# Reordered start, paired score staging and an earlier fold in an attention and max-out kernel on one Trainium2 core

## The chip, the cores and the metric

The kernel runs on one core of a Trainium2 chip. TensorE (PE, with its weight loads shown as PEld) does the matmuls and transposes, VectorE (DVE) and ScalarE (ACT) read their results out of PSUM, GpSimd (POOL) does some element-wise work and issues most transfers, and SyncE (SP) issues the transposing transfers. The metric is the device time of one execution in microseconds; a kernel's time is the median of its runs.

## The reference

For each of four batches, 32 inducing vectors attend to 12,544 rows of x, and the rows then attend to the 32 results. A max-out layer follows.

```python
def mab(q, kv):
    s = scale * (q @ kv.transpose(0, 2, 1))
    s = s - s.max(-1, keepdims=True)
    a = np.exp(s)
    a /= a.sum(-1, keepdims=True) + 1e-09
    return a @ kv
h = mab(I, x)          # x: (4, 12544, 128), I: (4, 32, 128)
y = mab(x, h)          # then flattened to (50176, 128)
out = np.maximum(y @ w1, y @ w2) @ w_out     # w1, w2: 128 x 1024, w_out: 1024 x 128
```

The kernel uses max(a, b) = a + relu(b - a): the part y @ w1 @ w_out goes through one 128 x 128 product w1out = w1 w_out, and only relu(y @ (w2 - w1)) is made in full width. As y is a mixture of the 32 rows of h, both are applied to h first (hwd = h (w2 - w1), m1 = h w1out), and each row of x only mixes 32 rows of these.

## The kernel before, in words

A batch is 98 column groups of 128 rows. **The start** handles batch 0 in eight units (five of 16 groups, one of 2, two of 8): `load_unit` loads a unit as float16, `u_transpose` transposes it on PE (line 194), `u_scores` makes the scores against the inducing vectors (210) and their exp (219), and `u_accum` adds the unit into two PSUM banks, h (234) and the row sums (244). `keep_warm` issues matmuls without use on a buffer of zeros. `prep_w1T` transposes w1 (610) and copies it out (616). `u_h` reduces the sums, takes the reciprocal and makes hT (255, 260, 262). The differences w21 = w2 - w1 are four subtractions (659). Then `small_hwd` makes hwd (354) and `prep_w1out` makes w1out (622).

**The steady part** is one list of bursts, 49 for a batch. The rows of a batch are cut into blocks of 16 groups and some smaller ones: batch 0 has blocks of 2, 4, 8, five times 16, and 4 groups, the others six of 16 and one of 2. A block of 16 takes eight bursts. `Block.stage` makes the exp of a block's scores against h, called e: four matmuls on column quarters of the array (409) and an activation (419). `Part.burst` makes four banks of relu inputs with matmuls on row quarters (474), which DVE (505) or ACT (509) evict as relu, and may open the next finals (489). `Part.final` multiplies relu with w_out (545, sometimes opened by 536), DVE scales by the denominator (561), and every second final issues an output transfer from POOL (569). `dens` makes denominators (430, 439).

Beside the bursts of batch b the sums of batch b + 1 are prepared: `p1_scores` (277, 286) and `p1_accum` (299, 309 or 312 on DVE; 316 or 319 on POOL, into eacc), then `small_fold` (324, a reduction of eacc on DVE), `small_h` (335 on PE, 338, 340), `small_hwd` (354) and `small_m1` (374).

The order on every engine is written out by hand: each engine runs its instructions in the order in which this program emits them. A small planner (`Model`) keeps estimated times of PE, DVE and ACT and chooses which of DVE and ACT evicts a bank and which of the eight PSUM banks is used. Its choices fix what is emitted and change nothing while the kernel runs. Work beside the bursts is tied to burst numbers by `at(g, f, ...)`, and a block is staged three bursts before its first burst.

Of the kernel before, what the change touches and what calls it, by code (L numbers as in the profile page):

```python
# [51 lines left out]
def kernel(  # L52
# [9 lines left out]
    nc = tc.nc  # L62
    B, N, C = x.shape
    M = inducing.shape[0]
# [12 lines left out]
        units += [(i, g, min(step, n - g)) for g in range(0, n, step)]  # L77
    units = units[:-3] + units[-1:] + units[-3:-1]
    NU = len(units)
    W_AT = NU - 3  # L80

    consts = ctx.enter_context(tc.tile_pool(name="consts", bufs=1))
    big = ctx.enter_context(tc.tile_pool(name="big", bufs=1))
# [11 lines left out]
    model = Model()  # L95
    uid = [0]

    def bank(shape, dtype=F32):
        i = model.bank()
        uid[0] += 1  # L100
        return i, psum.tile(shape, dtype, name=f"ps{uid[0]}", tag=f"bank{i}", bufs=1)
# [8 lines left out]
    def xn_of(b, i):  # L110
        return xn_tiles[(NP1 * b + i) % NXN]

    def load_x(b, i):
        k0, n = p1_blocks[i]
        nc.gpsimd.dma_start(out=xn_of(b, i)[:, 0:n, :], in_=xr[b, :, k0 : k0 + n, :])  # L115

    def load_unit(i):
        t, g, n = units[i]
        k0 = p1_blocks[t][0] + g
        nc.gpsimd.dma_start(out=xn_of(0, t)[:, g : g + n, :], in_=xr[0, :, k0 : k0 + n, :])  # L120
# [21 lines left out]
    identity16 = consts.tile([128, 128], F16, name="identity16")  # L142
    identity32 = consts.tile([128, 128], F32, name="identity32")
# [6 lines left out]
    w1f, w2f = wf[:, 0, :], wf[:, 1, :]  # L150
# [6 lines left out]
    with tc.manual_schedule(engines={ET.PE, ET.DVE, ET.Activation, ET.Pool, ET.SP}):  # L157
# [1 line left out]
        nc.vector.memset(warm, 0.0)  # L159
        nc.vector.memset(ones32, 1.0)  # L160
        nc.vector.memset(ones16, 1.0)
        load_unit(0)
        make_identity(nc, identity16)
        make_identity(nc, identity32)
        for i in range(1, NU):
            if i == W_AT:
                nc.gpsimd.dma_start(out=w1f, in_=moe_w1)
            load_unit(i)
        nc.gpsimd.dma_start(out=w2f, in_=moe_w2)
        nc.gpsimd.dma_start(out=woutp, in_=moe_w_out.rearrange("(jb j) c -> j jb c", j=128))  # L170

        def keep_warm(k):
            bi, ps = bank([128, 512])
            for _ in range(k):
                nc.tensor.matmul(out=ps, lhsT=warm[:, 0:128], rhs=warm, start=True, stop=True)
                end = model.pe(0.215, model.bank_free[bi])
            model.bank_free[bi] = end
# [5 lines left out]
        pool0 = {}  # L183

        def u_transpose(i):
            t, g0, n = units[i]
            xn = xn_of(0, t)
            step = 8 if n == P1B else 4
            for g in range(g0, g0 + n, step):
                m = min(step, g0 + n - g)  # L190
                bi, ps = bank([128, 8, 128], F16)
                end = 0.0
                for j in range(m):
                    nc.tensor.transpose(ps[:, j, :], xn[:, g + j, :], identity16)  # L194
                    end = model.pe(0.056)
                k = p1_blocks[t][0] + g
                dst = xT_tiles[0][:, k : k + m, :]
                if (g // step) % 2 == 0:
                    nc.vector.tensor_copy(out=dst, in_=ps[:, 0:m, :])  # L199
                    model.bank_free[bi] = model.ev("DVE", 64 * m, end)  # L200
                else:
                    nc.scalar.copy(out=dst, in_=ps[:, 0:m, :])  # L202
                    model.bank_free[bi] = model.ev("ACT", 128 * m, end)
# [21 lines left out]
        def u_accum(i):  # L225
            t, g, n = units[i]
            et = pool0.pop(("et", i))
            xn = xn_of(0, t)
            if i == 0:
                for name in ("h", "sum"):  # L230
                    pool0[name] = bank([128, 512])
                    model.bank_free[pool0[name][0]] = 1e9
            for j in range(n):
                nc.tensor.matmul(  # L234
                    out=pool0["h"][1][:, 0:M],
                    lhsT=xn[:, g + j, :],
                    rhs=et[:, j, :],
                    start=(i == 0 and j == 0),
                    stop=(i == NU - 1 and j == n - 1),
                )  # L240
                model.pe(0.025)
            for j in range(0, n, 4):
                w = min(4, n - j) * M
                nc.tensor.matmul(
                    out=pool0["sum"][1][:, 0:w],
                    lhsT=ones16,
                    rhs=et[:, j : j + w // M, :],
                    start=(i == 0 and j == 0),
                    stop=(i == NU - 1 and j + 4 >= n),
                )  # L250
                model.pe(0.056)

        def u_h():
            rec = smp.tile([C, M], F32, name="hrec_0", tag="hrec")
            nc.vector.reduce_sum(
                out=rec,
                in_=pool0["sum"][1][:, 0 : 4 * M].rearrange("p (k m) -> p m k", k=4),
                axis=mybir.AxisListType.X,
            )
            nc.vector.reciprocal(out=rec, in_=rec)  # L260
            hT4 = smp.tile([C, 4, M], F16, name="hT4_0", tag="hT4")
            nc.vector.tensor_mul(  # L262
                hT4,
                pool0["h"][1][:, None, 0:M].broadcast_to((C, 4, M)),
                rec[:, None, :].broadcast_to((C, 4, M)),
            )
            end = model.ev("DVE", 256 + 128, model.t["PE"], 0.2)
            for name in ("h", "sum"):
                model.bank_free[pool0[name][0]] = end
            st[0]["hT4"] = hT4.rearrange("c q m -> c (q m)")  # L270
# [302 lines left out]
        def blocks_of(b):  # L573
            sizes = [16] * (K // 16)
            rest = K - sum(sizes)
            while rest:
                s = 8 if rest >= 8 else 4 if rest >= 4 else 2
                sizes.append(s)
                rest -= s
            if b == 0:  # L580
                sizes = [2, 4, 8] + sizes[:-1]
                sizes[-1] = K - sum(sizes[:-1])
                last = sizes.pop()
                while last:
                    s = 8 if last >= 8 else 4 if last >= 4 else 2
                    sizes.append(s)
                    last -= s
            assert sum(sizes) == K
            res, k0 = [], 0
            for s in sizes:  # L590
                res.append(Block(b, k0, s))
                k0 += s
            return res
# [11 lines left out]
        def prep_w1T():  # L605
            for g in range(2):
                bi, ps = bank([128, 512])
                for j in range(4):
                    jb = 4 * g + j
                    nc.tensor.transpose(  # L610
                        ps[:, 128 * j : 128 * (j + 1)],
                        w1f[:, 128 * jb : 128 * (jb + 1)],
                        identity32,
                    )
                    end = model.pe(0.12, model.bank_free[bi])
                nc.scalar.copy(out=w1T[:, 4 * g : 4 * g + 4, :], in_=ps)
                model.bank_free[bi] = model.ev("ACT", 512, end)
# [16 lines left out]
        for i in range(last):  # L634
# [5 lines left out]
            keep_warm(1)  # L640
        u_scores(last - 1)
        u_accum(last - 2)
        prep_w1T()
        u_transpose(last)
        u_transpose(last + 1)
        u_accum(last - 1)
# [6 lines left out]
        u_accum(last + 2)  # L653
        for i in range(NXN - NP1):
            load_x(1, i)
        for i in range(4):
            eng = nc.vector if i < 2 else nc.gpsimd
            sl = slice(256 * i, 256 * (i + 1))
            eng.tensor_sub(w21[:, sl], w2f[:, sl], w1f[:, sl])
        for i in range(NXN - NP1, NP1):  # L660
            load_x(1, i)
        u_h()
        keep_warm(2)
        flat = [blk for b in range(B) for blk in blocks_of(b)]
        parts = [p for blk in flat for p in blk.parts]
        seq = [(p, u) for p in parts for u in range(p.nburst)]
        first = {}
# [2 lines left out]
            first.setdefault(p.blk.name, g)  # L670

        stages = {}
        for blk in flat:
            stages.setdefault(max(-1, first[blk.name] - 3), []).append(blk)
        stages[-1][0].stage()
        small_hwd(0)
        for blk in stages[-1][1:]:
# [5 lines left out]
        def at(g, f, *a):  # L683
            jobs.setdefault(g, []).append((f, *a))

        for b in range(B - 1):
            nb, g = b + 1, first[b]

            t0, l0 = (9, 24) if b == 0 else (-3, 16)
            at(g + t0, transpose_batch, nb)  # L690
            if nb + 1 < B:
                at(g + l0, hold_loads, nb)
            for i in range(NP1):
                s = g + (14 + 4 * i if b == 0 else 5 + 5 * i)
                at(s, p1_scores, nb, i)
                at(s + 2, p1_accum, nb, i)
                if nb + 1 < B:
                    at(g + l0 + 2 * i, load_x, nb + 1, i)
            for s, f in ((41, small_fold), (42, small_h), (43, small_hwd), (44, small_m1)):
                at(g + s, f, nb)  # L700

        queue = []
# [52 lines left out]
```

## Time and profile before

| | us |
|---|---|
| median of 9 runs | 349.05 |
| lowest and highest run | 348.19 and 351.48 |
| the profiled execution, its whole time | 351.33 |
| the profiled execution, span from the first to the last instruction | 349.2 |

All nine, in order: 348.19, 348.75, 348.84, 348.84, 349.05, 350.72, 350.95, 351.33, 351.48.

| engine | busy us in the span |
|---|---|
| PE | 335.8 |
| PEld | 267.6 |
| DVE | 302.1 |
| ACT | 270.3 |
| POOL | 95.5 |

In lines of the profile, times are microseconds from the first instruction; L12 is line 12 of the kernel before; `out<-in` names tiles without their numbers; x16 is a count of instructions, which can be a little short, as some records are missing. A timeline line gives start, duration, engine, line, operation, tiles and shapes, and in brackets idle time with what ended it. The chain of waits follows the last-ending work back from step to step. Matmuls overlap in the pipeline, so starts are compared with starts.

### The profile page before, as it was taken

The numbers are of one execution on the slowest core, as the hardware profiler recorded it, in microseconds if no ns is written. First come the engines' busy times: TensorE is split into PE (matmuls) and PEld (weight loads), VectorE is DVE, ScalarE is ACT, GpSimd is POOL, SyncE is SP. The second block draws the span as 40 slices with busy tenths as digits, with TensorE's granted clock in tenths as the row PEclk, the third lists the DMA queues.
The fourth block names the chain that finished last, engine by engine and source line by source line (L and its number), as shares of the span: only waits on it lengthen the run. The fifth ranks groups of instructions, "written<-read, shape, count | busy, mean of one in ns | idle before, by whom it ended". The sixth has DMA issues, their size and how long they took to land.

```text
span 349.2 us, 14492 instructions
## 1 busy us (share of the span) xinstructions
PE 335.8 (96%) x6349; PEld 267.6 (77%) x6349; DVE 302.1 (86%) x632; ACT 270.3 (77%) x519; POOL 95.5 (27%) x168
## 2 busy tenths in 40 slices
PE   7787999999999999999999999999999999999994
PEld 3775678888878788887777788887777778777774
DVE  2235899999999899999999999999999999999992
ACT  2465787777888887787888987787888889888980
POOL 6231112346412123544211222324211121111111
PEclk9896899999999999999999999999999999999999
DMA  7999559969947993997218992122212122222222
GB/s 117 232 244 215 133 133 258 197 158 195 213 145 136 222 256 100 179 226 205 92 71 164 254 206 94 68 88 92 92 65 92 77 92 92 95 92 92 93 94 105
DMA packets 51790, 50.42 MB, mean 144 GB/s; under 512 B 41456, under 2 KB 42000, under 8 KB 51728
## 3 DMA queue, kind: packets, MB, share of 16 engines
q0 software_dynamic: 13376, 39.85, 40.8%
q1 hardware_dynamic: 38352, 9.65, 17.0%
q8 instruction: 49, 0.80, 1.0%
q14 instruction: 13, 0.11, 0.1%
HBM read 27.28 MB, written 25.69 MB: 152 GB/s over the span
## 4 chain that ended last, share of the span: by engine, by line
PE 47%; issue 33%; POOL 9%; DMA 4%; DVE 4%; ACT 1%; POOLq 0%; ACTq 0%
PE ps L545 27%; PE ps L474 10%; POOL out_dram L569 7%; DMA xn<-in_x_dram 4%; DVE relu L505 2%; PE ps L489 2%; POOL eacc L319 2%; PE ps L277 1%; PE ps L409 1%; PE ps L299 1%; ACT relu L509 1%; PE ps L234 1%; PE ps L194 1%; DVE o L561 1%; DVE esum L324 1%
## 5 line engine op out<-in xcount | busy, mean ns | idle before, releaser
L509 ACT ACTIVATE relu<-ps 128x512 f16<-128x512 f32 x444 | 235.8, 601 | 47.7 <-PE ps L474 36.6
L505 DVE TENSOR_SCALAR relu<-ps 128x512 f16<-128x512 f32 x340 | 218.9, 680 | 6.5 <-PE ps L474 5.1
L545 PE MATMUL ps<-woutp,relu 128*128 128x128 f16 x3136 | 210.6, 221 | 0.0
L545 PEld LDWEIGHTS <-relu 128*128 128x128 f16 x3136 | 177.7, 98 | 28.7 <-issue 18.9
L569 POOL DMA_DIRECT2D out_dram<-o x100 | 54.4, 544 | 234.2 <-DVE o L561 170.5
L561 DVE TENSOR_TENSOR o<-ps,rp 128x256 f32<-128x256 f32 x196 | 82.0, 418 | 14.6 <-PE ps L545 11.2
L474 PE MATMUL ps<-e,hwd 32*128 32x256 f16 (+1 forms) x1632 | 83.4, 271 | 0.3
L474 PEld LDWEIGHTS <-hwd 32*128 32x128 f16 x1632 | 27.4, 93 | 19.1 <-issue 3.1
L489 PE MATMUL ps<-m,e 32*128 32x128 f16 x372 | 29.4, 214 | 0.4
L489 PEld LDWEIGHTS <-e 32*128 32x128 f16 x372 | 18.2, 92 | 6.7 <-issue 3.2
L319 POOL TENSOR_TENSOR eacc<-eacc,et 128x512 f32<-128x512 f32 (+1 forms) x18 | 18.5, 1029 | 0.3
L419 ACT ACTIVATE e<-ps 128x512 f16<-128x512 f32 (+2 forms) x30 | 16.3, 543 | 2.0 <-PE ps L409 2.0
L202 ACT COPY xT<-ps 128x1024 f16<-128x1024 f16 (+1 forms) x7 | 6.2, 890 | 12.9 <-PE ps L194 12.4
L199 DVE COPY xT<-ps 128x1024 f16<-128x1024 f16 (+2 forms) x8 | 4.5, 575 | 12.8 <-PE ps L194 12.7
L286 ACT ACTIVATE et<-ps 128x512 f16<-128x512 f32 (+1 forms) x21 | 11.4, 544 | 5.0 <-PE ps L277 5.0
L115 POOL DMA_DIRECT2D xn<-in_x_dram x21 | 11.5, 550 | 5.9 <-DMA xn<-in_x_dram 4.6
L409 PE MATMUL ps<-xT,hT 128*32 128x512 f16 (+2 forms) x120 | 11.2, 361 | 0.8 <-DVE hT L262 0.7
L194 PE MATMUL ps<-identity,xn 128*128 128x128 f16 x98 | 7.7, 238 | 3.3 <-DMA xn<-in_x_dram 3.0
L277 PE MATMUL ps<-inducingT,xT 128*128 128x32 f16 x294 | 10.6, 176 | 0.0
L299 PE MATMUL ps<-et,xn 128*128 128x32 f16 x294 | 10.6, 176 | 0.0
L194 PEld LDWEIGHTS <-xn 128*128 128x128 f16 x98 | 6.7, 107 | 4.6 <-DMA xn<-in_x_dram 4.2
L277 PEld LDWEIGHTS <-xT 128*128 128x128 f16 x294 | 9.6, 96 | 0.0
(65 smaller groups left out, 119.1 us busy)
## 6 DMA issues: line engine op xcount, KB each, us to landing
out_dram<-o POOLq DMA_DIRECT2D x96, 256.0 KB, 2.7
xn<-in_x_dram POOLq DMA_DIRECT2D x23, 512.0 KB, 8.6
wf<-in_moe_w_dram POOLq DMA_DIRECT2D x2, 512.0 KB, 14.2
xn<-in_x_dram POOLq DMA_DIRECT2D x2, 256.0 KB, 15.8
out_dram<-o POOLq DMA_DIRECT2D x4, 128.0 KB, 3.7
xT<-xn SPq DMA_TRANSPOSE x21, 6.3
xn<-in_x_dram POOLq DMA_DIRECT2D x4, 64.0 KB, 9.6
woutp<-in_moe_w_out_dram POOLq DMA_DIRECT2D x1, 256.0 KB, 12.5
```

The source lines that it names most:

```text
L194: nc.tensor.transpose(ps[:, j, :], xn[:, g + j, :], identity16)
L277: nc.tensor.matmul(out=ps[:, j * M : (j + 1) * M], lhsT=xT_tiles[b % 2][:, k0 + j, :], rhs=inducingT, start=True, stop=True,)
L319: nc.gpsimd.tensor_add(out=acc, in0=acc, in1=et[:, 0:n, :])
L409: nc.tensor.matmul(out=ps[32 * q : 32 * (q + 1), 0 : self.width], lhsT=st[self.b]["hT4"][:, 32 * q : 32 * (q + 1)], rhs=xT[:, q % self.g], ...
L419: nc.scalar.activation(out=self.e2[:, 0 : self.width], in_=ps[:, 0 : self.width], func=AF.Exp, scale=scale,)
L474: nc.tensor.matmul(out=ps[:, jj * w : (jj + 1) * w], lhsT=st[blk.b]["hwd"][r, 128 * jb : 128 * (jb + 1)], rhs=blk.e2[r, 128 * self.t0 : 12 ...
L489: nc.tensor.matmul(out=part.fin[q][1][:, 128 * s : 128 * (s + 1)], lhsT=part.blk.e2[r, 128 * tt : 128 * (tt + 1)], rhs=st[part.blk.b]["m1" ...
L505: nc.vector.tensor_scalar(out=dst, in0=src, scalar1=0.0, scalar2=None, op0=ALU.max)
L509: nc.scalar.activation(out=dst, in_=src, func=AF.Relu)
L545: nc.tensor.matmul(out=o, lhsT=self.relu[:, jb, q, tt, :], rhs=woutp[:, jb, :], start=False, stop=(s == 1 and jb == NJB - 1),)
L561: nc.vector.tensor_mul(self.osb[:, h : h + 2, :], ps[:, 0:256].rearrange("p (s c) -> p s c", s=2), rp.broadcast_to((128, 2, 128)),)
L569: nc.gpsimd.dma_start(out=outr[blk.b, :, k : k + nst, :], in_=self.osb[:, 0:nst, :])
```

## The change

The start: all eight units of x are loaded ahead of w1, w2 and w_out, where w1 had stood ahead of the last three units. The two identities are made after the third load is issued, not after the first. `u_accum` issues the sums' matmuls ahead of the h matmuls. `prep_w1T` moves from before the last three units to behind `u_h`, in the place of two warm-up matmuls, which are dropped. `u_h` moves ahead of the subtractions and of the later loads, and three of the four subtractions are on POOL instead of two.

The steady part: blocks are staged in pairs, both three bursts before the first burst of the first of them; the first three blocks of batch 0 stay single. `small_fold` is tied to burst 40 of a batch instead of 41.

```diff
-    W_AT = NU - 3
...
-        load_unit(0)
-        make_identity(nc, identity16)
-        make_identity(nc, identity32)
-        for i in range(1, NU):
-            if i == W_AT:
-                nc.gpsimd.dma_start(out=w1f, in_=moe_w1)
+        for i in range(NU):
             load_unit(i)
+            if i == 2:
+                make_identity(nc, identity16)
+                make_identity(nc, identity32)
+        nc.gpsimd.dma_start(out=w1f, in_=moe_w1)
         nc.gpsimd.dma_start(out=w2f, in_=moe_w2)
...
         def u_accum(i):
...
-            for j in range(n):
-                nc.tensor.matmul(out=pool0["h"][1][:, 0:M], ...)
-                model.pe(0.025)
             for j in range(0, n, 4):
                 nc.tensor.matmul(out=pool0["sum"][1][:, 0:w], ...)
                 model.pe(0.056)
+            for j in range(n):
+                nc.tensor.matmul(out=pool0["h"][1][:, 0:M], ...)
+                model.pe(0.025)
...
         u_accum(last - 2)
-        prep_w1T()
         u_transpose(last)
...
         for i in range(NXN - NP1):
             load_x(1, i)
+        u_h()
         for i in range(4):
-            eng = nc.vector if i < 2 else nc.gpsimd
+            eng = nc.vector if i == 3 else nc.gpsimd
             sl = slice(256 * i, 256 * (i + 1))
             eng.tensor_sub(w21[:, sl], w2f[:, sl], w1f[:, sl])
         for i in range(NXN - NP1, NP1):
             load_x(1, i)
-        u_h()
-        keep_warm(2)
+        prep_w1T()
...
-        for blk in flat:
-            stages.setdefault(max(-1, first[blk.name] - 3), []).append(blk)
+        for b in range(B):
+            blks = [blk for blk in flat if blk.b == b]
+            lead_in = 3 if b == 0 else 0
+            for i, blk in enumerate(blks):
+                j = i if i < lead_in else i - (i - lead_in) % 2
+                stages.setdefault(max(-1, first[blks[j].name] - 3), []).append(blk)
...
-            for s, f in ((41, small_fold), (42, small_h), (43, small_hwd), (44, small_m1)):
+            for s, f in ((40, small_fold), (42, small_h), (43, small_hwd), (44, small_m1)):
                 at(g + s, f, nb)
```

More of the change, by code (lines that the diff above doesn't have):

```diff
@@ L232, in u_accum @@
                     model.bank_free[pool0[name][0]] = 1e9
-            for j in range(n):
[L234 to L240, printed above, removed]
-                model.pe(0.025)
             for j in range(0, n, 4):
@@ L251, in u_accum @@
                 model.pe(0.056)
+            for j in range(n):
+                nc.tensor.matmul(
+                    out=pool0["h"][1][:, 0:M],
+                    lhsT=xn[:, g + j, :],
+                    rhs=et[:, j, :],
+                    start=(i == 0 and j == 0),
+                    stop=(i == NU - 1 and j == n - 1),
+                )
+                model.pe(0.025)
         def u_h():
```

## The prediction

> **What bounds the kernel now.** I read the page first (shares and slices), then the granted clock in stretches, the chain of waits, and last the timelines of PE, DVE, ACT and POOL around each edited line.
>
> ```profile
> PE 335.8 (96%) x6349; PEld 267.6 (77%) x6349; DVE 302.1 (86%) x632; ACT 270.3 (77%) x519; POOL 95.5 (27%) x168
> PE   7787999999999999999999999999999999999994
> DVE  2235899999999899999999999999999999999992
> ACT  2465787777888887787888987787888889888980
> ```
>
> From the fifth slice on (35 us) PE is the bound, with DVE close behind. The first four slices are another regime: PE waits for x. The chain of waits shows the passage from one to the other.
>
> ```profile
> 18.84 1.07 PE ps L194 x16
> ...
> 22.30 0.88 PE ps L610 x8
> ...
> 26.64 0.39 ACT et L219
> ...
> 27.08 0.35 PE ps L234 x8
> 27.43 0.13 PE ps L244 x2
> ...
> 27.59 0.30 DVE hrec L255
> 27.91 0.36 DVE hrec L260
> ...
> 28.30 0.30 DVE hT L262
> ...
> 28.65 0.30 PE ps L409 x3
> ```
>
> The last wait for a transfer ends at 18.84, with the fifth tile of x. All after it is PE, ACT and DVE work in series: the eight transposes of w1 (L610) stand in this chain although nothing on it needs them yet, and the row sums (L244) come after the h matmuls (L234) although the DVE reduction (L255) needs only the sums. These are what the change can shorten.
>
> The granted clock, by stretch (first number after the window its length, then PE, PEld, DVE, ACT, POOL busy; the clock is the 1.00 or 0.50):
>
> ```profile
> 11.00:14.40 3.40, 3.16 (x41) 2.66 (x39) 1.26 (x2) 1.51 (x2) 1.01 (x2) 0.50 1.06 212
> 24.60:28.06 3.46, 2.26 (x47) 1.51 (x44) 2.02 (x5) 1.37 (x4) 3.10 (x6) 1.00 1.07 213
> 28.06:31.50 3.44, 2.85 (x36) 1.77 (x36) 1.35 (x4) 1.47 (x5) 0.00 (x0) 0.50 1.07 216
> ```
>
> After a thin stretch before 28.06 the clock falls to half, and in the windows that follow it stays there to 38.3, 10.2 us.
>
> In the steady part the PE timeline gives the price of a staging (L409):
>
> ```profile
> 275.85 0.40 PE L474 MATMUL ps<-e,hwd 32*128 32x256 f16 x8
> 276.18 0.40 PE L409 MATMUL ps<-xT,hT 128*32 128x512 f16 x4
> 276.51 1.07 PE L545 MATMUL ps<-woutp,relu 128*128 128x128 f16 x16
> ```
>
> Start to start, burst to stage is 0.33 us, stage to final 0.33, and a burst followed at once by a final is 0.33 too (279.02 to 279.35), so one staging adds 0.33 us.
>
> **Part 1, loads and identities.** The four POOL instructions of the identities (0.22 + 0.29 + 0.20 + 0.29, 1.93 to 3.02) move behind two load issues; these two leave 1.0 us sooner, the rest as before. The identities then end near 4.1, and PE first uses one at 6.63, behind 18 warm-up matmuls: hidden, with 2.5 us to spare. Do earlier issues bring x sooner? From 4 us on the DMA share is 0.96 or more in every 2 us stretch (0.73 in 2 to 4, where the first tile starts), and the first tile, 5.3 us to landing, is still in flight until 6.5 while the second was issued at 2.97. The queue isn't starved. Ends: 0 and -1.0; I take 0, by the full DMA rows. w1 (0.5 MB) moves behind the last three x units. Bytes up to w2 are the same, so w2 still lands near 24 (POOL's wait for it ended at 24.18); w1 lands at about 23 instead of 20, and PE wants it at 26.7. x units 5 to 7 come up to 1.2 us sooner (w1's share, 18.8 to 20.0), but PE is behind its data there. Value: 0.
>
> **Part 2, prep_w1T behind u_h, sums first.** L610 leaves the chain: -0.88. et of the last unit is then ready at 26.16 instead of 27.04; sums 26.20 to 26.33, h until 26.68, and prep_w1T fills PE until 26.68 + 0.88 = 27.56. DVE starts at 26.36, and its three steps took 1.01 (27.59 to 28.60): hT at 27.37. The first staging now waits for PE, not for hT: 27.59 against 28.64, together -1.05. The two w1T casts (1.07 us on ACT for both) go ahead of the first e; I work out e ready at about 27.6 + 0.6 + 0.3 = 28.5, against 29.3 before, so they hide. keep_warm(2), 0.43 us of PE in the hT wait, costs nothing to drop. If the clock should be half at that time already, the transposes take 1.76 and the gain falls to about 0.2; if the DMA end of part 1 came in, it would be 2.0.
>
> **Part 3, w21.** Three subtractions on POOL (0.72 each) from 24.2 end at 26.4, then the four load_x issues (0.54 each) leave 0.7 later than before; three tiles are queued ahead of them, so no gap. One subtraction on DVE, 0.41 (free) to 0.91 (beside POOL), follows hT; the fourth small_hwd matmul needs it and comes 0.3 + 3 x 0.12 or more after hT. Between 0 and +0.3; I take 0.
>
> **Part 4, pairs.** 512 columns stream in 0.22 us (one warm-up matmul in the chain: 20.93, 0.22), so of the 0.33 of a staging 0.11 is the change into and out of column mode. A pair pays that once. Pairs: three in each of four batches, 12 (the first three blocks of batch 0 and each last block of two tiles stay single): 12 x 0.11 = -1.3. Against it stands the second exp, 0.54 to 0.61 on ACT in the same burst. After a single staging the first three batches mostly show no wait on PE (197.38: the next burst and its lead follow at 0.23 and 0.21, the least there is); the last shows about 0.06 in the next burst (277.75 to 278.02, 0.27 against 0.21 elsewhere) and up to 0.15. DVE has no gap there, ACT gaps of 0.30 to 0.42 a burst. I take +0.1 for each of the last batch's three pairs: -1.0 in all. Ends: -1.3, and +0.24 a pair, rival D.
>
> **Part 5, fold one burst sooner.** In before PE waits for esum 0.35 at 179.47 and at 258.27, and 0.22 at 100.6. For batches 2 and 3 the last eacc addition (L319) is long done (173.07 for a fold at 178.30), so the fold (1.02 us) just goes ahead of one burst's evictions: the wait of 0.35 goes, and those evictions come 1.0 later, next in line to be waited for. I take -0.3 each. For batch 1 the fold now stands in the very step of the last p1_accum (DVE's timeline, then POOL's):
>
> ```profile
> 97.97 0.18 DVE L312 TENSOR_TENSOR hacc<-ps,hacc 128x32 f32<-128x32 f32 x1
> 98.07 0.68 DVE L505 TENSOR_SCALAR relu<-ps 128x512 f16<-128x512 f32 x1
> ...
> 99.43 1.03 DVE L324 TENSOR_REDUCE esum<-eacc 128x32 f32<-128x512 f32 x1
> ```
>
> ```profile
> 98.35 0.54 POOL L569 DMA_DIRECT2D out_dram<-o  x1 [2.45 <-DVE hacc L312]
> 98.91 0.32 POOL L319 TENSOR_TENSOR eacc<-eacc,et 128x64 f32<-128x64 f32 x1
> ```
>
> POOL must first issue the output transfer, then add eacc, until 99.23. DVE, free at 98.15, waits 1.1 us there, with an eviction and an output multiplication queued behind it whose banks PE wants for the burst at 100.9. It had 0.33 idle in before. I take +0.6 (between 0 and +1.1). Sum of the part: 0.
>
> **The clock.** The thin stretch shrinks from 3.6 us (25.06 to 28.65) to 2.5 (24.2 to 26.7), with the w1 transposes behind it. The row 11.00:14.40 is mostly transposes (L194), and the clock came back to 1.00 after it: they woke PE. The Trainium skill, "TensorE: Matmul & The Clock Gate", Part 4, says the opposite, that transposes don't count as busy for the gate. By the row the fall becomes no more frequent; by the rule the thin stretch lasts 3.4 us, without the two warm-up matmuls in it, and most executions fall. The nine times shown lie in two groups, 348.19 to 349.05 (five) and 350.72 to 351.48 (four); I read the groups as without and with the long half-clock stretch, some 2.3 us apart. By the rule the median would move up by about 2.3. I follow the row and leave the shares as they are.
>
> **Sum.** -1.05 - 1.0 + 0 = -2.05. The profiled execution took 351.33 (span 349.2 and 2.1 around it), 2.28 above the median, in the slower group: a like execution becomes 349.3, the median 349.05 - 2.05 = 347.0. About 0.5% (1.75 us) is what a measurement here can tell from no change: faster is under 347.3, slower over 350.8.
>
> **Rivals.** A, the sum above: 347.0, chance 0.45, with 0.28 of it under 347.3. B, all of it comes: pairs -1.3, folds -0.6 because DVE has slack at batch 1, and x 0.3 earlier: 349.05 - 3.25 = 345.8; for it ACT's idle share (busy 46.8 of 58 us from 117 to 175), against it the full DVE. 0.17. C, the clock falls in most executions: 347.0 + 2.3 = 349.3; for it the rule and the lost warm-up matmuls, against it the row. 0.18, mostly within 0.5%. D, slower: ACT becomes the bound behind each pair. The second exp of 0.54 finds only some 0.2 of gap, so PE waits 0.35 for banks (L489 or L474 of the next burst), net +0.24 a pair: -1.05 + 12 x 0.24 = +1.8, 350.9. It eats the saving from 0.11 of added wait a pair on, and makes the kernel slower beyond 0.5% from about 0.34. Against it: ACT's 77%. 0.20. That the change doesn't do what it says I don't expect: each order is written out by hand.
>
> **Numbers.** Faster: A 0.28, B 0.17, C 0.01: 0.46. Within: A 0.17, C 0.13, D 0.06: 0.36. Slower: C 0.04, D 0.14: 0.18. The range reaches just past B and D: 345.6 to 351.0.
>
> **What would show it.** Right: the fifth tile's transposes still at 18.8; hrec near 26.4; the first L409 near 27.6 right behind L610; pairs of eight L409 taking 0.55 start to start where two singles took 0.66; no PE wait before L335 in batches 2 and 3, and a DVE gap of about 1 us before L324 in batch 1. Wrong: x landing a microsecond earlier or later, a second L409 group that waits for a bank or again takes 0.33, a burst after a pair that starts over 0.2 late, or half clock before 27 us.

## The result

The changed kernel takes 346.79 us (median of 16 runs, 345.78 to 349.53); the kernel before, run beside it, 349.55 (53 runs, 348.09 to 352.43). The ratio is 0.9922, with a 95% interval of 0.9902 to 0.9942: 2.7 us faster, between 2.0 and 3.4. The forecast was 347.0 by a gain of 2.05 us. Clocks of the changed kernel are told below for 17 executions, one more than the median counts.

In the changed kernel lines stand a little higher: two fewer from line 162 on, so L407 is the staging that was L409, L472 the burst, L543 the final, L608 the w1 transposes, L559 the scaling, L322 the fold. In `u_accum` the sums are L233 and the h matmuls L242.

Its profiled execution took 347.08 us, with a span of 345.1. The shares of the engines are nearly as they were:

```profile
PE 331.1 (96%) x6347; PEld 265.0 (77%) x6347; DVE 298.4 (86%) x626; ACT 272.0 (79%) x524; POOL 96.2 (28%) x169
```

The planner chose a little differently: ACT evicts 449 of the 784 relu banks instead of 444 (447 with the pairs alone, 446 with the fold alone). What each part brings includes its own choices of this kind.

The chain of waits through the start (start, length, what):

```profile
4.59 13.03 DMA xn<-in_x_dram
...
17.67 1.07 PE ps L192 x16
...
25.02 0.29 PE ps L233 x2
...
25.33 0.30 DVE hrec L253
...
26.12 0.30 DVE hT L260
...
26.46 0.24 PE ps L407 x4
```

The fifth tile of x is there at 17.67 instead of 18.84: 1.17 us that the forecast did not count. That is one execution against one. Over all traces the tile comes between 18.18 and 18.92 in the four kernels with the old loads, and between 17.51 and 17.81 in the seven with the changed kernel's, so some 1.0 us sooner. From its transposes to the first staging it was 9.81 us and is 8.79, -1.02, where -1.05 was forecast. The w1 transposes are gone from the chain before hT.

The granted clock in the same region (length, busy PE, PEld, DVE, ACT, POOL, then the clock, the busy share of the DMA engines and GB/s):

```profile
24.50:27.80 3.30, 2.72 (x38) 2.11 (x37) 2.03 (x6) 2.18 (x7) 2.18 (x5) 1.00 1.07 215
27.80:31.20 3.40, 2.46 (x54) 1.62 (x52) 2.75 (x6) 3.16 (x8) 0.00 (x0) 1.00 1.06 214
31.20:34.60 3.40, 3.35 (x48) 2.77 (x46) 2.40 (x5) 2.27 (x6) 0.56 (x1) 0.51 1.06 213
34.60:38.00 3.40, 3.29 (x59) 1.98 (x57) 2.60 (x6) 3.08 (x8) 0.19 (x1) 0.99 1.07 218
```

This execution has 3.4 us of half clock, after a wait of PE for m1d near 30 us, where that of before had 10.2 us. In this region two executions differ by their clock as well as by their kernel.

After about 45 us the profiled executions repeat each other to about 0.03 us unless the program differs (one exception stands at the order alone, below), so the rest is read from the starts of the same DVE scalings (lead is before minus after):

| scaling, about | before | after | lead |
|---|---|---|---|
| start of batch 0's long blocks | 45.94 | 42.33 | 3.61 |
| ahead of the first fold | 97.64 | 93.48 | 4.16 |
| behind it | 104.62 | 101.48 | 3.14 |
| batch 2 | 200.73 | 197.04 | 3.69 |
| last batch | 277.68 | 273.96 | 3.72 |
| last | 344.43 | 340.27 | 4.16 |

Of the first 3.61, 1.17 is the fifth tile and 1.02 the order; most of the rest is the clock. In what follows one step stands out: 1.02 us are lost at the first fold. The timelines of DVE and POOL there:

```profile
93.81 0.18 DVE L310 TENSOR_TENSOR hacc<-ps,hacc 128x32 f32<-128x32 f32 x1
95.09 1.03 DVE L322 TENSOR_REDUCE esum<-eacc 128x32 f32<-128x512 f32 x1 [1.10 <-POOL eacc L317]
```

```profile
94.19 0.54 POOL L567 DMA_DIRECT2D out_dram<-o  x1 [2.46 <-DVE hacc L310]
94.74 0.32 POOL L317 TENSOR_TENSOR eacc<-eacc,et 128x64 f32<-128x64 f32 x1
```

DVE stands still for 1.10 us until POOL has issued a transfer and added eacc.

### The profile page after: what moved, and what is told of

Read it like the earlier page. It is cut to its first block, busy times and chain, and to the rows that moved or that the text cites. A ratio compares the mean times of both kernels' runs of the same rounds, so it can differ in the third digit from the quotient of the medians.

```text
span 345.1 us, 14489 instructions
## 1 busy us (share of the span) xinstructions
PE 331.1 (96%) x6347; PEld 265.0 (77%) x6347; DVE 298.4 (86%) x626; ACT 272.0 (79%) x524; POOL 96.2 (28%) x169
## 4 chain that ended last, share of the span: by engine, by line
PE 62%; issue 23%; POOL 6%; DMA 4%; DVE 3%; ACT 1%; POOLq 0%; ACTq 0%; DVEq 0%
PE ps L543 37%; PE ps L472 13%; POOL out_dram L567 5%; DMA xn<-in_x_dram 4%; PE ps L487 3%; PE ps L297 2%; PE ps L275 2%; PE ps L407 2%; DVE relu L503 1%; ACT relu L507 1%; PE ps L192 1%; POOL xn L119 1%; DVE o L559 0%; PE ps L534 0%; PE ps L352 0%
## 5 line engine op out<-in xcount | busy, mean ns | idle before, releaser
L503 DVE TENSOR_SCALAR relu<-ps 128x512 f16<-128x512 f32 x335 | 216.0, 680 | 5.1 <-PE ps L472 4.0
L543 PE MATMUL ps<-woutp,relu 128*128 128x128 f16 x3136 | 210.1, 220 | 0.0
L543 PEld LDWEIGHTS <-relu 128*128 128x128 f16 x3136 | 177.3, 98 | 29.6 <-issue 20.0
L559 DVE TENSOR_TENSOR o<-ps,rp 128x256 f32<-128x256 f32 x196 | 82.0, 418 | 15.9 <-PE ps L543 12.6
L472 PE MATMUL ps<-e,hwd 32*128 32x256 f16 (+1 forms) x1632 | 83.1, 270 | 1.0 <-DVE relu L503 0.3
L472 PEld LDWEIGHTS <-hwd 32*128 32x128 f16 x1632 | 27.2, 92 | 19.7 <-issue 4.1
L487 PE MATMUL ps<-m,e 32*128 32x128 f16 x372 | 30.3, 214 | 1.3 <-DVE relu L503 0.5
L417 ACT ACTIVATE e<-ps 128x512 f16<-128x512 f32 (+2 forms) x30 | 14.8, 546 | 0.0
L192 PE MATMUL ps<-identity,xn 128*128 128x128 f16 x98 | 6.6, 219 | 3.3 <-DMA xn<-in_x_dram 3.1
L297 PEld LDWEIGHTS <-xn 128*128 128x128 f16 x294 | 9.5, 96 | 0.0
L192 PEld LDWEIGHTS <-xn 128*128 128x128 f16 x98 | 5.6, 97 | 4.6 <-DMA xn<-in_x_dram 4.3
```

The source lines that it names most:

```text
L297: nc.tensor.matmul(out=ps[:, 0:M], lhsT=xn[:, j, :], rhs=et[:, j, :], start=(j == 0), stop=(j == n - 1),)
L417: nc.scalar.activation(out=self.e2[:, 0 : self.width], in_=ps[:, 0 : self.width], func=AF.Exp, scale=scale,)
L472: nc.tensor.matmul(out=ps[:, jj * w : (jj + 1) * w], lhsT=st[blk.b]["hwd"][r, 128 * jb : 128 * (jb + 1)], rhs=blk.e2[r, 128 * self.t0 : 12 ...
L487: nc.tensor.matmul(out=part.fin[q][1][:, 128 * s : 128 * (s + 1)], lhsT=part.blk.e2[r, 128 * tt : 128 * (tt + 1)], rhs=st[part.blk.b]["m1" ...
L503: nc.vector.tensor_scalar(out=dst, in0=src, scalar1=0.0, scalar2=None, op0=ALU.max)
L543: nc.tensor.matmul(out=o, lhsT=self.relu[:, jb, q, tt, :], rhs=woutp[:, jb, :], start=False, stop=(s == 1 and jb == NJB - 1),)
```

## Experiments: one part alone

These four start from the kernel before and make one part of the change each.

**Identities behind the third load** (w1 stays ahead of the last three units).

```diff
-        load_unit(0)
-        make_identity(nc, identity16)
-        make_identity(nc, identity32)
-        for i in range(1, NU):
+        for i in range(NU):
             if i == W_AT:
                 nc.gpsimd.dma_start(out=w1f, in_=moe_w1)
             load_unit(i)
+            if i == 2:
+                make_identity(nc, identity16)
+                make_identity(nc, identity32)
```

> The kernel before with one edit: the two identities are made after the third x load is issued, not after the first; w1 stays ahead of the last three units. Theory (found from the trace after: the fifth tile of x was there at 17.67 and not at 18.84): the gap of 1.04 us between the first and second issue costs the transfers 1.2 us, so the transposes of the fifth tile start near 17.7 and the time falls by 1.2 us, ratio 0.9966. Rival (the prediction's value): the queue isn't starved, the fifth tile stays at 18.8, ratio 1.000; then the gain came from w1 leaving its place ahead of the last units.

Measured: 349.71 us (12 runs), ratio 0.9990 (0.9961 to 1.0019), so the 1.2 us expected don't show in the time. They do in the trace. The transposes of tiles 2 to 5 of x on PE, before first, then in this kernel:

```profile
10.34 1.33 PE L194 MATMUL ps<-identity,xn 128*128 128x128 f16 x16 [1.91 <-DMA xn<-in_x_dram]
...
12.76 1.83 PE L194 MATMUL ps<-identity,xn 128*128 128x128 f16 x16 [0.24 <-DMA xn<-in_x_dram]
...
18.84 0.84 PE L194 MATMUL ps<-identity,xn 128*128 128x128 f16 x12 [0.88 <-DMA xn<-in_x_dram]
```

```profile
8.84 1.07 PE L194 MATMUL ps<-identity,xn 128*128 128x128 f16 x16 [0.17 <-DMA xn<-in_x_dram]
...
11.26 1.07 PE L194 MATMUL ps<-identity,xn 128*128 128x128 f16 x16 [0.74 <-DMA xn<-in_x_dram]
...
17.06 1.07 PE L194 MATMUL ps<-identity,xn 128*128 128x128 f16 x16 [1.03 <-DMA xn<-in_x_dram]
```

In these two executions the second tile comes 1.5 us sooner and the fifth 1.8. So the earlier issue of two loads alone moves x. The landings in all traces say the same. From the first tile to the second it is 3.5 to 3.8 us in the four kernels with the identities between these two issues, and 2.4 to 2.5 in the ten without. The third and the fourth tile follow at 2.4 to 2.5 in every trace, the fifth at 3.2 to 3.9.

Busy time and transfers in two stretches of 2 us, before first, then in this kernel (the last two numbers are the busy share of the DMA engines and GB/s):

```profile
6.00:8.00 2.00, 1.72 (x21) 1.17 (x19) 0.80 (x8) 0.00 (x0) 1.25 (x3) 1.00 0.96 154
8.00:10.00 2.00, 0.43 (x5) 0.10 (x2) 0.50 (x1) 1.01 (x1) 0.00 (x0) 1.00 1.01 190
```

```profile
6.00:8.00 2.00, 1.72 (x17) 1.04 (x16) 0.61 (x7) 0.00 (x0) 1.26 (x3) 1.00 1.04 209
8.00:10.00 2.00, 1.83 (x37) 1.50 (x34) 1.20 (x2) 1.07 (x2) 0.54 (x1) 1.00 1.08 217
```

The engines are busy in all four rows, and move a quarter less between 6 and 8 us in the kernel before. Why the time doesn't show it: 6 of its 12 executions had a mean granted clock of 0.987 or less, where 16 of 63 of before had. Its three executions at 0.997 took 347.05 to 347.66, those of before at 0.997 took 347.96 to 348.88, about 1.0 us more. Whether the earlier x makes the clock fall more often without the new order behind it, or the 12 were a poor draw, stays open.

**The order at the end of the start**: prep_w1T, sums first, u_h and the subtractions as in the change, loads and identities as before. The new order in `u_accum`, the same as in the change, is left out of this cut.

```diff
         u_accum(last - 2)
-        prep_w1T()
         u_transpose(last)
...
+        u_h()
         for i in range(4):
-            eng = nc.vector if i < 2 else nc.gpsimd
+            eng = nc.vector if i == 3 else nc.gpsimd
...
-        u_h()
-        keep_warm(2)
+        prep_w1T()
```

> The kernel before with the order at the end of the start alone: prep_w1T behind u_h in the place of the two warm-up matmuls, the sums ahead of the h matmuls, u_h ahead of the subtractions, three of these on POOL; loads and identities as before. Theory: the first staging (L409) starts 1.05 us earlier than 28.65, near 27.6, and the time falls by 1.05 us plus what a rarer half clock brings (up to 0.6 us on the median): ratio 0.995 to 0.997. Rival: the w1 casts on ACT or the missing warm-up matmuls take it back, L409 earlier but the first final no earlier, ratio 1.000.

Measured: 347.41 us (20 runs), ratio 0.9951 (0.9931 to 0.9972), -1.7 us. The chain of waits:

```profile
18.92 1.07 PE ps L194 x16
...
26.58 0.30 DVE hrec L255
...
27.72 0.24 PE ps L409 x4
```

From the fifth tile to the first staging it is 8.80 us against 9.81: -1.01, as worked out. The interval of the time, -1.0 to -2.4, reaches this. The clock brings part of the rest: none of the 20 executions had a mean clock of 0.987 or less, 16 of 63 of before. It doesn't bring all: at 0.996 and more this kernel took 346.66 to 347.92 with a median of 346.9, before 348.4 in the median, 1.5 us more. What the other 0.5 is stays open. The profiled execution itself was a poor one (349.78): besides 3.4 us of half clock, PE stood still for 0.94 us at 83.0, with nothing in the profile to explain it, and the lead over before fell by 1.10 us there.

**Pairs alone.**

```diff
-        for blk in flat:
-            stages.setdefault(max(-1, first[blk.name] - 3), []).append(blk)
+        for b in range(B):
+            blks = [blk for blk in flat if blk.b == b]
+            lead_in = 3 if b == 0 else 0
+            for i, blk in enumerate(blks):
+                j = i if i < lead_in else i - (i - lead_in) % 2
+                stages.setdefault(max(-1, first[blks[j].name] - 3), []).append(blk)
```

> The kernel before with the blocks staged in pairs and nothing else. The prediction's value: 12 pairs save 1.0 us, ratio 0.997. Rival, from the aligned traces: a pair takes 0.55 instead of 0.67 start to start, but the wait for banks in the next bursts takes most of it back in all but the last batch, -0.4 us or less, ratio 0.999 to 1.000.

Measured: 348.51 us (20 runs), ratio 0.9973 (0.9950 to 0.9996), -0.9 us. In the last batch, PE's timeline:

```profile
284.61 0.40 PE L474 MATMUL ps<-e,hwd 32*128 32x256 f16 x8
284.93 0.62 PE L409 MATMUL ps<-xT,hT 128*32 128x512 f16 x8
285.48 1.07 PE L545 MATMUL ps<-woutp,relu 128*128 128x128 f16 x16
286.48 0.40 PE L474 MATMUL ps<-e,hwd 32*128 32x256 f16 x8
286.72 0.61 PE L489 MATMUL ps<-m,e 32*128 32x128 f16 x4
287.26 1.07 PE L545 MATMUL ps<-woutp,relu 128*128 128x128 f16 x16
```

The pair takes 0.55 start to start (284.93 to 285.48), two singles 0.67: the second group adds 0.22, the time in which 512 columns stream. Behind it L489 waits: 0.54 to the final instead of 0.21, so 0.33 more, where each single had cost up to 0.15. The profile names nothing that PE waits for there. ACT runs the two exps at that time:

```profile
286.48 1.11 ACT L419 ACTIVATE e<-ps 128x512 f16<-128x512 f32 x2
```

That PE waits for banks that ACT evicts later is likely by this, and not shown.

The scalings give the sum by batch, if the lead is always read when a batch's three pairs are done and the next batch's first pair is not yet staged. Ahead of all pairs it is 2.01: 1.79 (45.94 against 44.15) and 0.22 for the second group of the first pair, which stands ahead of that scaling here (37.15) and behind it in the kernel before (50.16). Then it is 2.35 (104.62, 102.27), 2.55 (185.21, 182.66), 2.80 (262.29, 259.49) and 3.03 (344.43, 341.40): +0.34, +0.20, +0.25 and +0.23, in all 1.0 us. The prediction's mechanism and its sum hold. Of the 0.12 of a pair, 0.36 a batch, 0.11 to 0.16 is taken back in each of the last three batches. That is less than the rival said, which had most of it taken back in all batches but the last.

**Fold alone.**

```diff
-            for s, f in ((41, small_fold), (42, small_h), (43, small_hwd), (44, small_m1)):
+            for s, f in ((40, small_fold), (42, small_h), (43, small_hwd), (44, small_m1)):
```

> The kernel before with the fold tied to burst 40 instead of 41 and nothing else. The prediction's value: 0, made of +0.6 in the first batch and -0.3 in each of the next two. Rival, from the aligned traces: +1.0 in the first batch, where DVE waits for eacc, and -0.4 in each of the next two, +0.2 in all; ratio 1.000 to 1.001 in either, so it is the times of the scalings before and after each fold that tell them apart.

Measured: 349.57 us (20 runs), ratio 1.0005 (0.9987 to 1.0024). The scalings: a lead of 2.92 ahead of the first fold (97.64 against 94.72, the lead itself from the start's clock), 1.96 behind it (116.89, 114.93), 2.07 and 2.01 behind the other two (188.61, 186.54; 265.86, 263.85). So -0.96 in the first batch, and between +0.11 and -0.06 in the others: not the -0.3 each of the prediction, nor the rival's -0.4. The alignment of the full change had mixed in what the pairs bring there. Where the 0.35 of PE's wait for the sums went shows at the second fold. PE in the kernel before, then PE and DVE in this one:

```profile
179.47 0.38 PE L335 MATMUL ps<-esum,ones 128*128 128x32 f32 x2 [0.35 <-DVE esum L324]
```

```profile
175.90 0.21 PE L489 MATMUL ps<-m,e 32*128 32x128 f16 x1
176.48 0.27 PE L489 MATMUL ps<-m,e 32*128 32x128 f16 x3 [0.37 <-DVE relu L505]
176.68 1.07 PE L545 MATMUL ps<-woutp,relu 128*128 128x128 f16 x16
177.58 0.36 PE L335 MATMUL ps<-esum,ones 128*128 128x32 f32 x2
```

```profile
174.88 0.94 DVE L324 TENSOR_REDUCE esum<-eacc 128x32 f32<-128x512 f32 x1
175.74 0.68 DVE L505 TENSOR_SCALAR relu<-ps 128x512 f16<-128x512 f32 x1
```

L335 starts 0.90 after the final with no wait, but ahead of that final PE waits 0.37 for a bank whose eviction (175.74) now stands behind the fold on DVE. The wait only moved.

## Experiments: one part of the change undone

**First fold at 41**, the others at 40; run twice.

```diff
-            for s, f in ((40, small_fold), (42, small_h), (43, small_hwd), (44, small_m1)):
+            for s, f in ((41 if b == 0 else 40, small_fold), (42, small_h), ...):
```

> The changed kernel with the first batch's fold back at burst 41, the others at 40. Theory: all of the fold's cost is the wait of DVE for eacc in the first batch (1.1 us in the trace after); undone, the times of the scalings after it come 0.9 to 1.0 us earlier and the time falls from 346.8 to about 345.9, ratio to the kernel before 0.9895. Rival (the prediction's size): 0.6 us or less, ratio above 0.9905.

> The changed kernel with the first batch's fold back at burst 41, again: 0.8 to 1.0 us under the changed kernel, ratio to the kernel before 0.989. Rival: the four earlier times were a lucky draw of clocks and it is within 0.3 us of the changed kernel.

Measured: 345.66 us (4 runs), ratio 0.9862 (0.9818 to 0.9905), and 346.10 (6 runs), 0.9889 (0.9854 to 0.9924). Beside the first, and beside the three experiments below that have 4 runs, the kernel before had 350.15 us in only 7 runs, where it has 349.5 to 349.6 in sets of 18 to 63, so these four ratios may be some 0.002 too low. The changed kernel beside the second:

> The changed kernel again, beside the three below on one chip: 346.8 us, ratio 0.992; its first staging (L407) near 26.4 and half clock, if any, after 30 us.

347.12 us (13 runs), ratio 0.9927 (0.9901 to 0.9953). So the second is 1.0 us under the changed kernel beside it. In the two traces the lead over the changed kernel rises at the fold by 0.85 and by 0.90 us (between its scalings at 93.48 and 113.88).

The trace of the changed kernel here missed its expectation: the clock fell at 25.6 us, in the thin stretch, the w1 transposes took 1.84 us instead of 1.07, and the first staging started at 27.25. From the fifth tile to that staging it is 9.44 us then, so the new order gains 0.37 in such an execution, where the prediction's aside had about 0.2.

**First fold at 40, the addition a burst sooner.**

```diff
-                at(s + 2, p1_accum, nb, i)
+                at(s + (1 if (b, i) == (0, NP1 - 1) else 2), p1_accum, nb, i)
```

> The changed kernel with the fold left at burst 40, and the last p1_accum of the first batch one burst sooner, at 39. Theory: the loss is DVE waiting for eacc, and the addition being queued on POOL behind an output transfer in the same burst; with the addition a burst ahead DVE's gap of 1.1 us before the fold goes, and most of the 0.8 us with it. Rival: the loss comes from the fold's 1.02 us standing ahead of that burst's evictions, wait or not; then the times after the fold stay within 0.2 us of the changed kernel's.

Measured: 345.78 us (6 runs), ratio 0.9876 (0.9842 to 0.9910). DVE:

```profile
92.27 0.13 DVE L310 TENSOR_TENSOR hacc<-ps,hacc 128x32 f32<-128x32 f32 x1
...
94.01 1.02 DVE L322 TENSOR_REDUCE esum<-eacc 128x32 f32<-128x512 f32 x1
```

No idle time stands before the fold. The lead over the changed kernel is 0.07 before the moved addition, -0.20 behind it (93.68 against 93.48) and +1.10 behind the fold (100.38 against 101.48), so 1.0 us in all. The fold still goes first, ahead of the next burst's evictions; it was the wait for eacc, not the fold's own 1.02 us, that cost the time.

**w1 ahead of the last three units.**

```diff
         for i in range(NU):
+            if i == NU - 3:
+                nc.gpsimd.dma_start(out=w1f, in_=moe_w1)
             load_unit(i)
```

> The changed kernel with the w1 load back ahead of the last three x units. Theory (the prediction's value): 0, since PE reaches the last units after their data in either order; the first staging (L407) stays within 0.2 us of 26.5. Rival: w1 ahead makes the last units late by 1.2 us, and the start loses up to 1 us, ratio to the kernel before 0.995.

Measured: 346.16 us (4 runs), ratio 0.9893 (0.9849 to 0.9937), no slower than the changed kernel's 0.9922 and 0.9927. Its profiled execution had half clock from 25.1 to 28.5, so its first staging at 26.82 is no fair reading. Up to the reduction of the sums the clock was full: from the fifth tile (17.33) to hrec (24.99) it is 7.66 us, as in the changed kernel (17.67 to 25.33). The last units are not late, and the rival is out. The fifth tile itself is even sooner in the two kernels with w1 ahead of the last three units (17.33, and 17.06 with the identities alone) than in the seven with the changed kernel's loads (17.51 to 17.81). Loading all of x ahead of every weight brought nothing that can be seen here, and may have cost a few tenths.

**Identities ahead of all loads.**

```diff
+        make_identity(nc, identity16)
+        make_identity(nc, identity32)
         for i in range(NU):
             load_unit(i)
-            if i == 2:
-                make_identity(nc, identity16)
-                make_identity(nc, identity32)
```

> The changed kernel with both identities made ahead of the first load, so that all eight loads are issued in a row, 1.04 us later than the first three are in the changed kernel. Theory: what cost time in before was that the second tile was issued after the first one's packets had begun; issued in a row the tiles land 2.45 us apart, and the fifth one 1.0 us later than in the changed kernel, near 18.6: +1.0 us, ratio 0.995. Rival: the identities delayed the making of the first transfer's descriptors; then the fifth tile lands near 17.6 or sooner and the ratio is 0.992.

Measured: 346.48 us (4 runs), ratio 0.9895 (0.9859 to 0.9931), at clocks of 0.998 to 1.000. POOL's waits for the landing of the first, second and third tile of x show the spacing:

```profile
7.27 0.54 POOL L165 DMA_DIRECT2D wf<-in_moe_w_dram  x1 [1.10 <-DMA xn<-in_x_dram]
9.71 0.53 POOL L166 DMA_DIRECT2D wf<-in_moe_w_dram  x1 [1.91 <-DMA xn<-in_x_dram]
12.15 0.90 POOL L167 DMA_DIRECT2D woutp<-in_moe_w_out_dram  x1 [1.91 <-DMA xn<-in_x_dram]
```

2.44 us from tile to tile, as after, where before had 3.8 from the first (5.3 to landing after its issue at 1.25) to the second (10.3). The fifth tile's transposes start at 18.22, 0.55 later than in the changed kernel and 0.6 sooner than before. So the loss in before is not a late start: here the first load is issued 0.5 later than in before (1.77), and still the second tile lands sooner. What costs is the gap between the first and the second issue, or POOL's work in it, which no run tells apart. The same work between the third and the fourth issue costs nothing: in the changed kernel POOL makes the identities there (2.97 to 4.10), and the fourth tile lands 2.48 behind the third. The times of this kernel (346.34 to 347.03) lie within the changed kernel's at the same clocks (345.78 to 347.07), so less was lost than the 1.0 expected.

## Experiments: the clock

**Warm-up matmuls in the last units.**

```diff
         u_scores(last + 1)
+        keep_warm(2)
         u_accum(last)
         u_accum(last + 1)
         u_scores(last + 2)
+        keep_warm(2)
         u_accum(last + 2)
```

> The changed kernel with two warm-up matmuls (0.43 us) in each of the two places where PE waits for the exp of the last units. Theory: it is the thin stretch of PE work there that makes the clock fall; with it filled, hardly any execution shows a mean clock under 0.99 (4 of 17 in the changed kernel), the slow tail near 349 goes, the median falls by 0.2 to 0.5 us. Rival: the clock falls by the phase of its windows and later gaps as well, the tail stays, and the four matmuls cost up to 0.3 us: no faster than the changed kernel.

Measured: 346.47 us (4 runs, clocks 0.994 to 1.000), ratio 0.9892 (0.9854 to 0.9930). Its profiled execution still had half clock, from 30.3 to 33.7. Filling the thin stretch doesn't stop the fall that comes later; four runs can't show whether the tail is gone.

**The same, with four more ahead of the first final, and the first fold at 41.**

```diff
                 small_m1(0)
+            if g == 1:
+                keep_warm(4)
             if queue:
```

> The changed kernel with the first batch's fold at 41, and warm-up matmuls in the waits of PE: two and two in the thin stretch of the last units, and four ahead of the first final, where PE waits for m1d. Theory: the half clock that still comes near 31 us follows from that second wait; filled, no execution shows half clock before the end and the median is 0.3 us under the one with the fold alone, about 345.5. Rival: the half clock stays, or the eight matmuls cost as much as they bring.

Measured: 345.72 us (6 runs, 345.33 to 345.89), ratio 0.9878 (0.9842 to 0.9914). Its clock:

```profile
24.50:27.80 3.30, 3.15 (x44) 2.17 (x45) 2.02 (x6) 2.27 (x7) 2.67 (x5) 1.00 1.06 212
27.80:31.20 3.40, 3.12 (x56) 1.97 (x56) 2.75 (x6) 3.16 (x8) 0.00 (x0) 1.00 1.06 213
31.20:34.60 3.40, 3.23 (x66) 2.32 (x64) 2.83 (x8) 2.63 (x7) 0.56 (x1) 1.00 1.07 216
```

The stretch from 27.8, with 3.12 us of PE instead of 2.46, no longer ends in half clock, and all six executions have 0.996 or more; in the profiled one the rest is the end of the program. The six times lie within 0.6 us; the changed kernel's 13 beside them within 2.7. That the added matmuls are the reason is not shown beyond doubt: the kernel with the identities ahead of all loads has 0.998 to 1.000 in its four executions without them. This version, the one with the addition a burst sooner (345.78) and the first fold at 41 (345.66 in its first four runs) are the fastest, and noise covers their differences. The first two together weren't run.

## Why the prediction was right, and where not

| part | predicted us | shown us | by |
|---|---|---|---|
| identities behind the third load | 0 | about -1.0 (fifth tile) | all traces of either order |
| w1 behind the last units | 0 | no loss to undo it, perhaps a small cost | w1 ahead |
| order behind the last unit | -1.05 | -1.01 to -1.02 | order alone; after |
| w21 on POOL | 0 | not seen | order alone |
| pairs | -1.0 | -0.9 in time, -1.0 in trace | pairs alone |
| fold, first batch | +0.6 | +0.96 alone, +1.02 after | fold alone; after |
| fold, two others | -0.6 | about 0 | fold alone |
| clock | 0 | no more long half-clock stretches | executions' clocks |
| sum | -2.05 | -2.7 (-2.0 to -3.4) | ratio |

The terms that are shown, -1.0 - 1.0 - 1.0 + 1.0, make -2.0, at the edge of the ratio's interval. The clock can account for much of the rest: the long stretch cost 2.5 us in the profiled execution of before (its lead of 2.92 behind the fold alone, less 0.42 for the fifth tile), and 16 of 63 executions had one, which makes up to 0.6 us on the mean, an estimate. That the forecast of 347.0 came close to 346.79 is luck in good part: the loads gave 1.0 that was not counted, and the fold took 1.0 that was not counted.

**Loads: the step that failed.** "The queue isn't starved ... I take 0, by the full DMA rows." The rows were full and said nothing of the rate. In before the second tile took 3.8 us from the first one's landing to its own, while the engines showed as busy; the third and the fourth took 2.4 to 2.5. A share of busy time counts packets in flight, and slow ones fill it as well: 0.96 at 154 GB/s, 1.04 at 209. The number that spoke stood at the end of the same row: 154 GB/s in 6 to 8 us and 190 in 8 to 10, against 203 in 4 to 6 and 209 in 10 to 12. The bound of -1.0 was named and not chosen.

**Order: right in size.** L253 was forecast for 26.4 with x at 18.84; with x at 17.67 it is at 25.33. The last wait is another one than forecast: the first staging was to wait for PE, and in the chains of the changed kernel and of the order alone it waits for hT, which ends at 26.42, 0.02 behind the w1 transposes. DVE's three steps took 1.09 instead of 1.01.

**Pairs: right in mechanism and sum, not by batch.** 0.55 against 0.67 was measured as forecast. The forecast was 0.33 for each of the first three batches and next to nothing for the last; measured are 0.34, 0.20, 0.25 and 0.23. The wait behind a pair is there in the last batch (0.33), but it stands in the place of two waits of singles, up to 0.15 each; in the second and third batch waits that the prediction put at nothing take about 0.1 a batch.

**Fold: mis-sized both ways.** In the first batch the wait of DVE was worked out right (1.1), and what reaches the end was put at 0.6 for an idle time that DVE had elsewhere; nearly all of it, 0.96, came through. In the other two "the wait of 0.35 goes" was right and the gain of 0.3 wrong: the prediction said itself that the evictions are next in line to be waited for, and gave them nothing. They cost what the fold gave.

**Clock: the row was the better guide than the rule, as far as these runs go.** By the Trainium skill's rule in "TensorE: Matmul & The Clock Gate", Part 4, transposes wouldn't count and low clocks would become more frequent. The long half-clock stretch went away instead. A mean clock of 0.987 or less, which takes some 9 us of half clock, stands in 35 of 140 executions of the kernels with the old order at the end of the start (16 of 63, 4 of 18 and 2 of 7 of before, 13 of 52 with the identities, the pairs or the fold alone), and in none of 84 with the new one (30 of the changed kernel, 34 of its variants, 20 of the order alone). What share the transposes have in it, and what the shorter stretch, no run here separates. That the share would stay the same was wrong. Shorter falls stayed: 14 of the 30 executions of the changed kernel have 0.988 to 0.995, and half clock before 27 us, a sign of wrong in the prediction, came in two traces (25.6 in the changed kernel's second, 25.1 with w1 ahead). A fall through the wait for m1d near 30 us was not in the prediction at all; the changed kernel and most of its variants show it.

**The rivals.** D did not come: a pair's added wait stays under what the pair saves, in every batch. C did not come either. B had the loads' direction right, with 0.3 of the 1.0, and took the first fold for free, which cost 1.0.

## What to carry to other kernels

Read the rate of a transfer, bytes by landing time, not the busy share of its queue, and issue the first loads back to back. Before a step is moved one burst forward on an engine, look at what it reads and which queue the writer of that is in: here an addition behind an output transfer on POOL cost more than the early reduction could give. A wait that goes from one instruction is only gone if no other in the same engine's queue inherits it.

## What the runs showed of the hardware

A second load whose issue began 1.04 us after the first one's had ended, some 0.5 us after the first one's packets had begun to move, landed 3.5 to 3.8 us behind it in four traces. Issued right after it, it landed 2.4 to 2.5 us behind, in all ten traces with that order. Why is not known from these runs; issuing the first load 0.5 us later (identities first) kept the short spacing, and the same gap ahead of the fourth load cost nothing.

Two stagings in a row on PE took 0.55 us where two apart took 0.67.

In the starts of these fourteen traces the half clock lasts 3.41 us or three times that, 10.24, and begins at different times from execution to execution. Cut on these steps of 3.41 us, the stretches at full clock that it came behind have 1.5 to 2.6 us of PE work, so they are thin and not idle. The amount alone doesn't decide: 2.17 us with the order alone (15.2 to 18.6) and 2.29 with the fold alone (24.1 to 27.5) were followed by full clock. Behind 2.7 us or more at full clock it came in none of them.
